# A transformer block on one core: crossed halves of k^T v by transfer for two more batches, and a new order of work behind the first product of h

## The chip, the core and the metric

The kernel runs on one core of a Trainium2 chip. A core has a matrix engine (PE, with weight loads counted apart as PEld), a vector engine (DVE), a scalar engine (ACT), a general engine (POOL) and a queue processor (SP). Each engine works through its own queue strictly in order, and waits for others by semaphores. The metric is device time of one execution in microseconds (us), less is better.

## What is computed

For 8 batches with 8 heads, 576 positions and 64 columns per head:

```
kv  = k^T v                       (64 x 64 per head)
o   = q kv;  x = o / sqrt(mean(o^2) + 1e-6) * g      (x: 576 x 512 per batch)
h   = relu(x @ w_in)              (576 x 1024)
c   = conv over 3 neighbouring positions of h, one weight per column and tap
out = (h * sigmoid(c)) @ w_out    (576 x 512)
```

Inputs and output are float32 in device memory.

## The kernel before

Work is done in bf16, transposed: columns on the 128 partitions, positions along the free dimension. A pair of heads makes one tile t of 0 to 3; the 1024 columns of h are 8 tiles f. The steps below have the names that the kernel gives them; a name with numbers, such as oq.4.0, is the step for batch 4, tile 0.

- **Lq, Lk, Lv** (line 304), **Li**, **Lo**: loads of q, k, v and of both weight matrices, all on POOL's queue, converted on the way.
- **kv** (361): k^T v of a batch on PE, into one bank of PSUM. **kvc** (batches 0, 1) copies it into a block-diagonal tile.
- For batches 2 to 7 the product q kv is made in quarters of PE's array (**oq**, 467). It needs k^T v twice: as it is (**kvn**, a copy from PSUM) and with the halves of the partitions crossed (kvx). The crossed tile is made either by **ky**, two copies from PSUM on ACT or DVE (457), or by **kx**, two transfers on SP's queue out of kvn (452), 32 KB each. Before, batches 2 to 5 use ky, batches 6 and 7 use kx.
- q is transposed on PE (**qt**, **qtp**) and copied from PSUM (**qc**) for batches 0 to 4, and by a DMA transpose on SP's queue (**dq**, 439) for 5 to 7.
- **sq** squares o on ACT; **oc** copies o out of PSUM. The mean of squares comes from a product with ones or selectors (**on**, **ss**), the root from ACT (**nl**, **ln**, 587). For batches 2 to 5 the root is split into two bf16 parts (**sl**) and spread by PE (**sp**, 606); for 6 and 7 it goes through device memory (**fw** writes it, **fr** reads it back broadcast, 613 and 620). **mu**, **mu0** and **muh** on DVE multiply o by root and g, giving x.
- **hm** (643): one tile of h, 8 matmuls of 288 columns; for batches 0 and 1 some are cut in two parts (**ha**, **hb**). **re** is the relu out of PSUM, on ACT or DVE.
- **ta**, **aa**, **ab** (702 to 715): the convolution on DVE. **sg** (748) is the sigmoid on ACT, **mg** (754) multiplies h by it on DVE. Two tiles of h of batch 0 go through PE instead (**dg**, **cm**).
- **om**, **oh** (764, 781): the product with w_out, in tiles of 128 rows and for the first and last pair of batches in two halves of f; **ea**, **eh** copy it out of PSUM on ACT or DVE, **st**, **sh** store it on SP's queue.
- **unread**: matmuls whose result nobody reads; they fill gaps of PE.

Sigmoid and root live in different tables of ACT, and a change of table is an instruction of its own (217); the order holds 12 of them.

The order is written out by hand: a string ORDER of 697 words, which a loop at the end of the kernel runs through one by one, emitting the instructions of each. Each engine's queue has them in just that order, fixed by dependencies from each instruction to the one before it on its engine. In a word, what stands behind `@` are the slots of the buffers that the step takes (PSUM has eight banks, 0 to 7; most products take two that follow each other), and `:1` picks the other engine of a copy or relu:

```
hm.2.4@0  re.2.4      first banks 0 and 1, relu on ACT
re.3.4:1              relu on DVE
```

For re, kvn, ky, oc and ea the plain form is ACT and `:1` DVE; for qc it is the other way round. So a word that is moved, or that takes another slot, changes which wait comes first and who is behind it. A step waits for its inputs, and for the last readers of the slots that it takes.

Of the kernel before, what the change touches and what calls it, by code (L numbers as in the profile page):

```python
# [67 lines left out]
pre@0,0,0 Lq.1.0@1 unread.10.0@1 qt0.0.0@0 qt0.0.1@1 ca.k.0:1 pi ca.v.0:1 qc0.0.0:1@0 unread.2.2@2
kv.0.0.1@3 pn kv.0.1.1@2 kvc.0.0.1.0:1@0 kvc.0.0.1.1 kvc.0.1.1.1 qc0.0.1 unread.3.4@0 kvc.0.1.1.0 ot.0.1@4 ct@1
unread.1.3@0 sq.0.1@0 pg Li.1 unread.2.1@2 on.0.1@0 ot.0.0@6 qt0.0.2@2 pc Li.3 nl.0.1@0 Lk.1.0@1 sq.0.0@0 al.x0@0  # L70
kv.0.2.1@3 kvc.0.2.1.0:1 kvc.0.2.1.1:1 unread.1.1@0 Lv.1.0@1 Li.0 mu0.0.1 on.0.0@0 qc0.0.2:1@0 nl.0.0@1 Lk.1.2 al.h0@0
qt0.0.3@3 ot.0.2@4 sq.0.2@0 kv.0.3.1@2,0 mu0.0.0 qc0.0.3:1 on.0.2@6 unread.3.2@1 kvc.0.3.1.0 kvc.0.3.1.1:1 nl.0.2@0
# [5 lines left out]
sq.1.2@0 sq.1.3@1 Lq.2.0@0 re.0.4 pl on.1.2@6 Lv.2.0@0 aa.0.0 on.1.3@4 nl.1.2@0 ab.0.0 mu0.1.2 nl.1.3@1 hm.0.5@6
qtp.2.0@0 mu0.1.3 re.0.5:1 ha.1.2@4 sg.0.1 hb.1.2 qc.2.0@0 ta.0.4@0 hm.1.6@2 sg.0.3 qtp.2.1@0 Lk.2.0@0 ta.0.5 aa.0.2
sg.0.0 hm.1.1@6 ab.0.2 re.1.2 qc.2.1@1 sg.0.2 ha.1.3@4 ta.1.2@3 re.1.1 sg.0.4 sg.0.5 hb.1.3 mg.0.0 re.1.6 hm.1.7@6  # L80
al.h1@1 kv.2.0.4@0 re.1.7 mg.0.1 re.1.3 kvn.2.0.4:1 ky.2.0.4.1 hm.1.0@2 hm.1.5@6 ky.2.0.4.0 re.1.0 ta.1.6@1 re.1.5
oq.2.0@0 oq.2.1@4 sq.2.0@0 sq.2.1@1 hm.1.4@2 mg.0.2 ta.1.7 ta.1.3 ta.1.0@0 oq.2.2@6 Lv.3.0@1 oc.2.0:1@0 aa.1.3 oc.2.1
oq.2.3@0 Lk.3.0@1 aa.1.1 Lq.3.0@1 kv.3.0.4@4 ta.1.1 sq.2.2@2 sq.2.3@3 ss.2@5 kvn.3.0.4:1 re.1.4 oc.2.2:1@1 qtp.3.0@2
Lo.0 oc.2.3 ky.3.0.4.1 ky.3.0.4.0 ln.8@0 qtp.3.1@0 qc.3.0@0 qc.3.1@1 oq.3.1@6 oq.3.0@2 ab.1.3 oq.3.2@0 sq.3.0@0
oc.3.0@2 aa.1.0 sq.3.1@1 sl.8@0 om.0.1.0@4 Lo.1 oc.3.1 al.x2@0 ab.1.1 sq.3.2@2 om.0.3.0@5 om.0.2.0@2 Lq.4.0@0 oq.3.3@6
ta.1.4@2 om.0.3.4 oc.3.2@3 sq.3.3@3 ta.1.5 om.0.1.4 ab.1.0 oc.3.3 sp.2.0@0,6 ss.3@3 ea.0.3@0 al.x1@1 om.0.0.0@5
ea.0.1@1 ln.1@0 mu.2.0.0 sp.2.1@0,3 sg.1.7 Lv.4.0@0 mu.2.0.1 Lk.4.0@0 om.0.0.4 mu.2.1.0 mu.2.1.1 sl.1@0 qtp.4.0@6
qc.4.0:1@0 hm.2.4@0 om.0.2.4 re.2.4 sg.1.6 sg.1.1 sp.3.1@6,3 sg.1.0 ea.0.0:1@2 mu.3.1.1 mu.3.1.0 Lq.5.0@1 hm.2.2@0
aa.1.2 kv.4.0.4@5 re.2.2 ea.0.2@3 Lv.5.0@1 kvn.4.0.4 sp.3.0@6,3 mu.3.0.1 hm.2.5@0 sg.1.3 mu.3.0.0 ab.1.2 hm.2.7@2
re.2.5 dq.5.0@2 re.2.7 hm.3.5@6 mg.1.0 mg.1.3 hm.3.4@0 ky.4.0.4.0 Lk.5.0@1 sg.1.2 hm.2.6@2 ky.4.0.4.1:1 oq.4.0@4  # L90
re.3.4:1 oq.4.1@0 sg.1.5 ta.2.4@0 re.3.5 dq.5.1@1 re.2.6 ta.2.5 sq.4.0@0 oc.4.0@0 hm.3.1@6 re.3.1 mg.1.1 hm.3.3@2
aa.2.2 qtp.4.1@4 sq.4.1@1 qc.4.1@0 hm.3.6@6 oc.4.1 sg.1.4 mg.1.2 om.0.8.0@0 oq.4.2@4 re.3.3 oq.4.3@2 Lq.7.0@0 re.3.6
Lv.7.0@0 kv.5.0.4@1 sq.4.2@2 oc.4.2@1 ab.2.2 hm.2.3@6 ta.2.6@2 kvn.5.0.4 sq.4.3@3 hm.3.7@4 oc.4.3 ky.5.0.4.0:1
Lk.7.0@0 hm.3.2@2 ky.5.0.4.1:1 sg.2.5 sg.2.4 re.3.7:1 oq.5.0@4 om.0.8.4 sq.5.0@4 om.0.6.0@1 re.2.3:1 oq.5.1@6 re.3.2:1
oc.5.0@2 oq.5.2@2 ea.0.8@4 oq.5.3@4 sq.5.2@5 om.0.4.0@0 oc.5.2@3 om.0.6.4 Lv.6.0@1 mg.2.2 ta.2.7 aa.2.3 om.0.4.4
sq.5.1@6 ss.4@2 oc.5.1 ta.2.2@0 sq.5.3@7 ss.5 om.0.5.0@3 om.0.5.4 hm.2.1@6 ea.0.6@5 ln.2@0 ea.0.4@6 ab.2.3 hm.2.0@0
oc.5.3 st.0.0 ta.2.3 sl.2@0 re.2.1 Lk.6.0@1 ea.0.5@2 aa.2.1 sp.4.0@4,6 mu.4.0.1 om.0.7.0@2 re.2.0 kv.7.0.4@3
sp.4.1@0,6 om.0.7.4 mu.4.0.0 hm.3.0@4 dq.7.0@3 sg.2.7 mu.4.1.1 mu.4.1.0 hm.4.6@6 al.h2@0 sg.2.6 re.3.0 ea.0.7@7
kvn.7.0.4 ab.2.1 mg.2.3 ta.2.0@2 hm.4.0@0 sp.5.0@2,4 kx.7.0.4.1 re.4.6 re.4.0 sg.2.2 hm.4.2@6 hm.4.4@0 mu.5.0.0
mu.5.0.1 ta.2.1 kx.7.0.4.0 st.0.5 re.4.2 st.0.1 Lq.6.0@1 hm.4.5@2 re.4.4 sp.5.1@4,6 re.4.5 kv.6.0.4@0 sg.2.3 oq.7.0@2  # L100
sq.7.0@0 mu.5.1.0 hm.4.3@4 dq.7.1@0 kvn.6.0.4 mu.5.1.1 oc.7.0@0 hm.5.0@6 hm.4.1@0 re.4.3 kx.6.0.4.0 kx.6.0.4.1 re.5.0
dq.6.0@1 re.4.1 oq.7.2@2 aa.2.0 mg.2.1 ab.2.0 sq.7.2@1 oq.7.1@4 oc.7.2:1@1 sg.2.1 sq.7.1@2 hm.5.2@6 hm.5.6@0 re.5.2:1
hm.5.3@2 al.x3@1 oc.7.1 re.5.6:1 dq.6.1@2 hm.5.5@6 oq.7.3@0 re.5.3:1 oq.6.0@2 re.5.5:1 sg.2.0 st.0.3 sq.7.3@3 hm.5.1@4
sq.6.0@4 mg.2.0 st.0.8 hm.5.4@6 oc.6.0@2 re.5.4 re.5.1 om.1.3.0@2 oc.7.3 ta.3.2@0 oq.6.1@4 ta.3.4@2 oq.6.2@6
ea.1.3:1@0 sq.6.1@5 oq.6.3@0 om.1.2.0@3 ta.3.3 sq.6.2@6 sq.6.3@7 ss.7@2 oc.6.2:1@3 ta.3.5 aa.3.1 oc.6.3:1 ss.6@6
st.0.7 om.1.7.0@7 ln.3@0 ab.3.1 oc.6.1 ea.1.2@1 sg.3.2 hm.4.7@4 sg.3.3 aa.3.2 fw.3 st.0.2 ln.4@0 om.1.6.0@6 re.4.7
om.1.4.0@0 ab.3.2 mg.3.1 om.1.8.0@1 hm.5.7@2 sg.3.4 om.1.1.0@4 ea.1.6@2 st.1.2 sg.3.5 fr.6.0@0 ta.3.0@0 om.1.0.0@5
# [10 lines left out]
ea.3.4:1@1 ea.3.0@0 om.3.6.4 st.2.0 om.3.5.4 om.3.3.4 om.3.2.4 st.3.4 st.3.0 ea.3.6:1@2 ea.3.5:1@3 oh.3.8.0@5 st.3.6
om.3.1.4 eh.3.8.0:1@4 st.2.5 ea.3.2@1 st.3.5 st.3.2 ea.3.3@2 st.3.3 om.3.7.4 ea.3.1@0 unread.1.2@0 sh.3.8.0 ea.3.7@0
st.3.1 st.3.7 oh.3.8.1 eh.3.8.1 sh.3.8.1  # L120
"""


# [1 line left out]
def kernel(  # L125
# [216 lines left out]
    def copy(to, fr, on_act):  # L342
        if on_act:
            nc.scalar.activation(to, fr, AX.Copy)  # L344
        else:
            nc.vector.tensor_copy(to, fr)  # L346
# [504 lines left out]
```

## Time and profile before

| | us |
|---|---|
| median of 3 runs | 176.29 |
| lowest and highest run | 176.2, 176.9 |
| span of the profiled execution, from its first to its last instruction | 174.7 |
| PE, DVE, ACT, POOL busy in it | 164.6, 151.8, 144.0, 30.8 |

The profile was taken from one execution of the program; its own time is known only as this span, and the timed runs stand 1.6 us above it. Busy time counts matmuls from start to modelled end, so that small gaps between them can hide in it. The granted clock of PE is full in all of the span but its start and end. DMA is busy until about 90 us, mostly with POOL's loads, and again in parts with stores.

### The profile page before, as it was taken

To read this page: it belongs to the slowest core of one execution; us is meant where nothing else is said; L and a number is where in the kernel's file an instruction comes from. 1 tells how busy PE (TensorE), PEld (TensorE's weight loads), DVE (VectorE), ACT (ScalarE), POOL (GpSimd) and SP (SyncE) were. 2 spreads that over 40 slices of the span, in tenths; PEclk is the share of its full clock that TensorE was granted. 3 is DMA by queue.
4 is the path that set the end of the run, shared out by engine and by line. 5 is a ranking of instruction groups with operands and counts; after the bars stand their busy time and mean duration, and the time that the engine had idled before them with its cause. 6 is when DMAs were issued, how large, how long until landed. Compare 5 with 4: busy or idle time off the path is not lost.

```text
span 174.7 us, 3978 instructions
## 1 busy us (share of the span) xinstructions
PE 164.6 (94%) x1590; PEld 100.1 (57%) x1607; DVE 151.8 (87%) x248; ACT 144.0 (82%) x224; POOL 30.8 (18%) x54
## 2 busy tenths in 40 slices
...
GB/s 151 182 186 198 200 202 203 205 204 204 208 203 205 203 204 164 162 196 191 190 203 234 72 261 6 149 188 181 173 268 161 152 0 4 23 277 235 90 322 196
DMA packets 37450, 30.81 MB, mean 176 GB/s; under 512 B 8608, under 2 KB 32952, under 8 KB 37432
## 3 DMA queue, kind: packets, MB, share of 16 engines
...
q8 instruction: 12, 0.20, 0.4%
...
## 4 chain that ended last, share of the span: by engine, by line
PE 76%; DVE 9%; DMA 4%; POOL 4%; ACT 2%; issue 2%; POOLq 0%; ACTq 0%
PE bank L764 35%; PE bank L643 30%; DMA w_in_sb<-in_moe_w_in_dram 4%; PE bank L361 3%; PE bank L467 2%; DVE taps L703 1%; DVE qT L346 1%; POOL q_sb L245 1%; DVE taps L709 1%; DVE h L754 1%; PE bank L606 1%; DVE taps L702 1%; POOL v_sb L245 1%; POOL k_sb L245 1%; PE bank L781 1%
## 5 line engine op out<-in xcount | busy, mean ns | idle before, releaser
L643 PE MATMUL bank<-xT,w_in_sb 128*128 128x288 bf16 x480 | 63.6, 286 | 0.3 <-ACT root L545 0.2
L764 PE MATMUL bank<-w_out_sb,h 128*128 128x512 bf16 x267 | 62.4, 379 | 0.8 <-issue 0.3
L643 PEld LDWEIGHTS <-w_in_sb 128*128 128x128 bf16 x480 | 46.0, 98 | 14.9 <-issue 1.6
L748 ACT ACTIVATE taps<-taps,cwn 128x1152 bf16<-128x1152 bf16 (+1 forms) x38 | 39.7, 1078 | 7.4 <-DVE taps L715 7.3
L764 PEld LDWEIGHTS <-h 128*128 128x128 bf16 x280 | 26.4, 98 | 31.0 <-issue 1.2
L649 ACT ACTIVATE h<-bank 128x576 bf16<-128x576 f32 x48 | 30.2, 656 | 3.0 <-PE bank L643 2.8
L344 ACT ACTIVATE row<-bank 128x512 f32<-128x512 f32 (+1 forms) x29 | 16.3, 595 | 8.8 <-PE bank L764 6.0
L754 DVE TENSOR_TENSOR h<-h,taps 128x2304 bf16<-128x2304 bf16 (+1 forms) x20 | 22.0, 1109 | 0.6 <-ACT taps L748 0.6
L709 DVE TENSOR_TENSOR taps<-taps 128x2304 bf16<-128x2304 bf16 (+1 forms) x19 | 21.5, 1134 | 0.2
L715 DVE TENSOR_TENSOR taps<-taps,h 128x2304 bf16<-128x2304 bf16 (+1 forms) x19 | 21.5, 1131 | 0.2
L496 ACT ACTIVATE sq<-bank 128x576 bf16<-128x576 f32 x28 | 17.8, 663 | 0.6 <-PE bank L467 0.3
L703 DVE TENSOR_SCALAR taps<-h,cwn 128x1152 bf16<-128x1152 bf16 (+1 forms) x38 | 17.8, 467 | 0.0
L702 DVE TENSOR_SCALAR taps<-h,cwn 128x1152 bf16<-128x1152 bf16 (+1 forms) x38 | 17.4, 457 | 0.3 <-ACT h L649 0.2
L217 ACT ACT_TABLE_LOAD x12 | 15.4, 1283 | 2.6 <-issue 2.4
L651 DVE TENSOR_SCALAR h<-bank 128x576 bf16<-128x576 f32 x16 | 11.8, 752 | 1.7 <-PE bank L643 0.8
L344 ACT ACTIVATE o<-bank 128x576 f32<-128x576 f32 x19 | 12.8, 674 | 0.0
L632 DVE SCALAR_TENSOR_TENSOR xT<-o,cw,bank 128x576 bf16<-128x576 f32 x16 | 12.2, 808 | 0.1
L304 POOL DMA_DIRECT2D q_sb<-in_q_dram x8 | 6.2, 770 | 30.2 <-PE bank L391 29.4
L430 PE MATMUL bank<-fill 128*128 128x512 bf16 x25 | 9.0, 481 | 1.5 <-DVE fill L232 1.5
L346 DVE COPY row<-bank 128x512 f32<-128x512 f32 (+1 forms) x8 | 5.4, 672 | 4.4 <-PE bank L781 2.4
L361 PE MATMUL bank<-v_sb,k_sb 96*64 96x64 bf16 x384 | 8.3, 197 | 0.7 <-ACT sq L496 0.5
L361 PEld LDWEIGHTS <-k_sb 96*64 96x64 bf16 x384 | 7.1, 112 | 2.9 <-issue 2.2
...
## 6 DMA issues: line engine op xcount, KB each, us to landing
...
q_sb<-in_q_dram POOLq DMA_DIRECT2D x4, 144.0 KB, 4.7
```

The lines of the kernel that those rows point to most:

```text
L344: nc.scalar.activation(to, fr, AX.Copy)
L361: nc.tensor.matmul(ps[i][i * D:(i + 1) * D, t - t0, :], k_sb[:, 2 * t + i, r * D:(r + 1) * D], v_sb[:, 2 * t + i, r * D:(r + 1) * D], star ...
L496: nc.scalar.activation(in_order(b, s), product(b, t), AX.Square)
L643: nc.tensor.matmul(ps[:, e, :HS], w_in_sb[:, t, f * P:(f + 1) * P], x[:, t, e * HS:(e + 1) * HS], start=(t == 0), stop=(t == NT - 1))
L649: nc.scalar.activation(to, fr, AX.Relu)
L702: nc.vector.tensor_scalar_mul(tap[:, 0, f % 2, :n, 8:8 + S], h[:, f], cwn[:, 0, f:f + 1])
L703: nc.vector.tensor_scalar_mul(tap[:, 1, f % 2, :n, :S], h[:, f], cwn[:, 2, f:f + 1])
L709: nc.vector.tensor_add(tap[:, 1, :, :n, :S], tap[:, 0, :, :n, 7:7 + S], tap[:, 1, :, :n, 1:1 + S])
L715: nc.vector.tensor_add(y, y, h[:, 2 * j:2 * j + 2])
L748: nc.scalar.activation(y, y, AX.Sigmoid, scale=cwn[:, 1, f:f + 1])
L754: nc.vector.tensor_mul(h, h, T["tap", c, j][:, 1, :, :n, :S])
L764: nc.tensor.matmul(T["om", p, m], h[:, f, m * P:(m + 1) * P], w_out_sb[:, f, :], start=(f == 0), stop=(f == NF - 1))
```

## The change

Batches 4 and 5 make their crossed tile by kx in place of ky. So the four copies go, and SP's queue has four more transfers of 32 KB. The tiles for kvn and kvx of all six batches are now allocated ahead of the steps, and no longer by the first kvn.

The order is the same in its first 69 words, up to the norm of the last tile of batch 0 (`nlh.0.3.1`). Behind that all 628 words are in a new order. Beside the four above, the same steps are in it, and PE has the same 1607 matmuls, 26 of them unread as before. The changes that the prediction speaks of:

- relus that go from DVE to ACT: re.0.2, re.0.3, re.2.3, re.5.3, re.7.0, re.7.2, re.7.6; from ACT to DVE: re.0.6, re.1.2, re.1.4;
- qc.2.1, kvn.2 and kvn.3 go from DVE to ACT; kvn.4, one half of ky.3 and one kvc of batch 1 from ACT to DVE;
- oc: 5.1, 6.1, 7.1 and 7.3 are on DVE, 6.2, 6.3 and 7.2 on ACT; of ea some go each way;
- st.0.0, st.0.1 and st.0.2, the first stores, stand ahead of dq.5.0 on SP's queue, and st.0.8 and st.0.6 ahead of kx.7; before, only st.0.0 is issued before kx.7, behind both dq.5;
- hm.6.5 stands behind the products of batch 7, among those of om.2; the squares of batch 6 stand in the order 0, 1, 3, 2, with both ss behind;
- oh.3.8.0 and oh.3.8.1 stand next to each other at the end; eh.3.8.0 is on ACT, eh.3.8.1 on DVE; one unread matmul is the last on PE.

```diff
 ORDER = """
...
-ot.0.3@2 sqh.0.3.0@0 mu0.0.2 qt.1.0@0 sqh.0.3.1 onh.0.3.0@6 qc.1.0@0 onh.0.3.1 nlh.0.3.0@1 nlh.0.3.1 ha.0.2@4
-muh.0.3.1 ha.0.3@0 muh.0.3.0 ps dg.6 Lv.1.2 hm.0.6@6 dg.7 hb.0.2 re.0.2:1 hm.0.7@2 hb.0.3 re.0.6 cm.0.6@4 sg.0.6@0
...
+ot.0.3@2 sqh.0.3.0@0 mu0.0.2 qt.1.0@0 sqh.0.3.1 onh.0.3.0@6 qc.1.0@0 onh.0.3.1 nlh.0.3.0@1 nlh.0.3.1 dg.7 Lv.1.2 dg.6
+muh.0.3.0 ps ha.0.2@4 ha.0.3@0 muh.0.3.1 hm.0.6@6 re.0.6:1 hb.0.2 hb.0.3 hm.0.7@2 re.0.7:1 re.0.2 ta.0.2@0 cm.0.6@4
...
+qtp.2.1@4 qc.2.1:1@0 al.h1@1 hm.1.1@2 re.1.1 sg.0.3 sg.0.2 qc.2.0@2 re.0.5:1 ta.0.5 aa.0.2 ab.0.2 sg.0.4 ha.1.2@6
+hb.1.2 re.1.2:1 ta.1.2@3 sg.0.0 Lv.2.0@0 mg.0.1 mg.0.0 hm.1.5@4 re.1.5 ha.1.3@2 hb.1.3 re.1.3 ta.1.3 aa.1.1 Lk.2.0@0
+kv.2.0.4@6 ky.2.0.4.1 ky.2.0.4.0 kvn.2.0.4 hm.1.6@0 re.1.6 ta.1.6@1 hm.1.7@2 re.1.7 ta.1.7 aa.1.3 oq.2.0@6 sq.2.0@2
...
+ea.0.2@6 st.0.2 om.0.0.4 ea.0.0@7 sl.1@0 sp.3.1@0,3 mu.3.1.1 mu.3.1.0 hm.2.2@6 re.2.2 Lv.4.0@0 Lk.4.0@0 kv.4.0.4@5
+sg.1.0 sg.1.3 aa.1.2 kvn.4.0.4:1 kx.4.0.4.0 kx.4.0.4.1 sp.3.0@6,0 Lq.5.0@1 sg.1.2 hm.2.7@2 sg.1.7 mu.3.0.1 mu.3.0.0
...
+om.3.1.4 ea.3.1@2 st.3.1 om.3.3.4 ea.3.3:1@1 st.3.3 oh.3.8.0@3 oh.3.8.1 eh.3.8.0@2 sh.3.8.0 eh.3.8.1:1 sh.3.8.1
+unread.1.2@1
...
 """
...
+    for b in QUAD:
+        T["kvn", b] = consts.tile([P, NT, D], BF16, name=f"kvn{b}")
+        T["kvx", b] = consts.tile([P, NT, D], BF16, name=f"kvx{b}")
+
     @op
     def kvn(b, t0, n):
-        if t0 == 0:
-            T["kvn", b] = consts.tile([P, NT, D], BF16, name=f"kvn{b}")
-            T["kvx", b] = consts.tile([P, NT, D], BF16, name=f"kvx{b}")
         copy(T["kvn", b][:, t0:t0 + n], T["kvps", b, t0][0], pick[0] == 0)
```

More of the change, by code (lines that the diff above doesn't have):

```diff
@@ L67 @@
 ORDER = """
[L68 to L72, printed above, removed]
@@ L78 @@
[L78 to L82, printed above, removed]
@@ L83 @@
[L83 to L107, printed above, removed]
@@ L118 @@
[L118 to L120 removed]
+pre@0,0,0 Lq.1.0@1 unread.10.0@1 qt0.0.0@0 qt0.0.1@1 ca.k.0:1 pi ca.v.0:1 qc0.0.0:1@0 unread.2.2@2 kv.0.0.1@3 pn
+kv.0.1.1@2 kvc.0.0.1.0:1@0 kvc.0.0.1.1 kvc.0.1.1.1 qc0.0.1 unread.3.4@0 kvc.0.1.1.0 ot.0.1@4 ct@1 unread.1.3@0
@@ new lines @@
+re.2.7 ab.1.2 st.0.0 hm.2.5@4 re.2.5 Lv.5.0@1 dq.5.0@2 hm.3.5@6 re.3.5 hm.3.4@2 sg.1.5 mg.1.3 mg.1.0 oq.4.0@0 sq.4.0@0
+oc.4.0@3 re.3.4:1 ta.2.4@0 ta.2.5 Lk.5.0@1 hm.2.6@6 oq.4.1@2 hm.3.3@4 qtp.4.1@0 re.2.6 sq.4.1@2 re.3.3 sg.1.4 mg.1.1
+dq.5.1@0 oc.4.1 hm.3.6@6 re.3.6 Lq.7.0@0 hm.3.1@4 re.3.1 qc.4.1@1 oq.4.3@2 oq.4.2@0 sq.4.2@1 kv.5.0.4@6 kvn.5.0.4
+kx.5.0.4.0 kx.5.0.4.1 mg.1.2 sq.4.3@3 oc.4.2@1 oc.4.3 aa.2.2 ab.2.2 sg.2.4 Lk.7.0@0 hm.3.7@4 re.3.7:1 ta.2.6@2 ta.2.7
+aa.2.3 hm.2.3@6 re.2.3 sg.2.5 om.0.8.0@0 hm.3.2@3 re.3.2:1 om.0.8.4 ea.0.8@7 oq.5.1@5 sq.5.1@4 oq.5.0@1 sq.5.0@6
@@ new lines @@
+om.0.6.0@7 om.0.4.0@0 oc.5.0@2 oc.5.1:1 oq.5.3@3 sq.5.3@5 al.x2@0 om.0.4.4 mg.2.2 ta.2.2@0 ta.2.3 ab.2.3 oq.5.2@1
+dq.7.0@1 st.0.8 Lv.7.0@0 sq.5.2@7 om.0.5.0@6 ss.4@5 ss.5 ln.2@0 sl.2@0 dq.7.1@2 aa.2.1 oc.5.2@0 oc.5.3 om.0.6.4
+ea.0.6@7 st.0.6 om.0.5.4 ea.0.5@6 hm.2.1@1 re.2.1 Lv.6.0@1 hm.2.0@4 sp.4.0@2,6 mu.4.0.0 ea.0.4@4 mu.4.0.1 re.2.0
+om.0.7.0@1 sg.2.7 sg.2.6 kv.7.0.4@0 kvn.7.0.4 kx.7.0.4.0 kx.7.0.4.1 sp.4.1@2,4 mu.4.1.1 mu.4.1.0 om.0.7.4 hm.3.0@6
+re.3.0 hm.4.6@2 al.h2@0 re.4.6 ea.0.7@7 hm.4.0@4 hm.4.5@2 re.4.0 ab.2.1 sg.2.2 mg.2.3 ta.2.0@2 sp.5.0@4,0 mu.5.0.1
```

46 lines of the change are left out of this document (32 added, 14 removed).

## The prediction

> **What bounds the kernel now.** I read the page's first lines, then the busy time in four stretches that I cut where the chain that ended last changes engine: the first product of h, the last normalised tile of batch 1, the first product of batch 2, the last gate.
>
> ```profile
> span 174.7 us, 3978 instructions
> PE 164.6 (94%) x1590; PEld 100.1 (57%) x1607; DVE 151.8 (87%) x248; ACT 144.0 (82%) x224; POOL 30.8 (18%) x54
> ```
> ```profile
> 16.60:31.60 15.00, 13.23 (x157) 9.29 (x160) 13.01 (x26) 13.09 (x27) 7.82 (x18) 1.00 1.34 202
> 31.60:56.50 24.90, 23.39 (x313) 15.29 (x314) 24.73 (x50) 24.70 (x41) 5.03 (x7) 1.00 1.30 205
> 56.50:167.60 111.10, 110.31 (x943) 66.55 (x952) 105.54 (x144) 93.29 (x135) 4.91 (x6) 1.00 0.75 161
> ```
>
> After the length of a stretch stand the busy us of PE, PEld, DVE, ACT and POOL, PE's clock and the DMA share. From 31.6 to 56.5 DVE is idle for 24.90 - 24.73 = 0.17 us and ACT for 0.20, while PE has gaps. From 56.5 to 167.6 PE is idle for 111.10 - 110.31 = 0.79 us in 111. So there are two regimes, and the chain of waits in order of time shows the same:
>
> ```profile
> 31.59 1.54 DVE xT L565 x2
> ...
> 47.29 0.75 DVE qT L346
> ...
> 56.50 0.98 PE bank L643 x8
> ...
> 124.15 13.81 PE bank L643 x112
> ...
> 147.52 10.74 PE bank L764 x49
> ...
> 171.36 0.28 ACT row L344
> ```
>
> Up to about 47 us nearly every piece of the chain is DVE's, from 56.5 on nearly every one PE's. The new order issues the same matmuls. Hence what it can gain is bounded: the 0.8 us of PE's gaps in the long second regime, and before it DVE's gaps: 2.0 us (15.00 - 13.01) and 0.17. Past 56.5 us, work taken from DVE or ACT shortens nothing unless it closes one of those 0.8 us.
>
> **The change, part by part.** *Copies that become transfers.* Four copies of crossed halves go, one from ACT and three from DVE; four transfers on SP come, two for batch 4 and two for batch 5.
>
> ```profile
> L344 ACT ACTIVATE kvx<-bank 64x256 bf16<-64x256 f32 x5 | 1.9, 378 | 0.1
> L346 DVE CAST kvx<-bank 64x256 bf16<-64x256 f32 x3 | 1.3, 420 | 0.1
> L346 DVE CAST kvn<-bank 128x256 bf16<-128x256 f32 x2 | 0.8, 414 | 0.0
> ```
> ```profile
> L452 SPq DMA_DIRECT2D kvx<-kvn x4: 467/568/589, 90.4 to 97.3; - x4
> ```
> ```profile
> kvx<-kvn SPq DMA_DIRECT2D x2, 32.0 KB, 3.0
> ```
> ```profile
> 59.65 0.95 PE L361 MATMUL bank<-v_sb,k_sb 96*64 96x64 bf16 x48
> ```
> ```profile
> 65.78 0.31 PE L467 MATMUL bank<-qT,kvn 64*64 64x288 bf16 x1
> ```
>
> That takes 3 x 0.42 us off DVE and 0.38 off ACT. All of it lies past 56.5 us, where PE hides them; I cost it at nothing. The price is a delay: the product oq.4.0 needs both transferred halves. They are issued after kvn.4 on DVE, which follows kv.4. That ended at 60.60 us (59.65 + 0.95) and will end near 60.9, with the later start of the second regime worked out below; behind one add on DVE kvn.4 then ends near 61.65. Two issues of 0.57 us put the second at 62.25. The 3.0 us are the landing of the pair of batch 7, issued between 90.4 and 91.0 with loads still running, so it lands near 65.25. The old oq.4.0 began at 65.78, with one product of h (0.98) more ahead of it and a wait of 0.2; PE will be there at 65.78 - 0.98 - 0.2 + 0.45 = 65.05. So it waits 0.2 to 0.3 us, with all of PE's queue behind it. Bounds: 0 if it lands as fast as the later pair (2.0), 4 us if it takes the 7.4 of the transposes that SP issued at 62 us under full load. I take 0.25, since copies of the same form are the nearest row.
>
> ```profile
> kvx<-kvn SPq DMA_DIRECT2D x2, 32.0 KB, 2.0
> ```
> ```profile
> qT<-q_sb SPq DMA_TRANSPOSE x2, 7.4
> ```
>
> The Trainium skill, "DMA: Bandwidth & Descriptors", section "Anatomy of one DMA", gives a fixed cost of some 2.0 us and bytes over 436 GB/s; by that, an estimate, 32 KB land 2.1 us after issue and this wait would be zero. The unloaded pair agrees with 2.0, the loaded pair differs with 3.0.
>
> *The first regime: same work, other waits.* Counting the order up to the last normalisation of batch 2, DVE loses two relus (re.0.2, re.0.3), one qT copy and two kvn to ACT, and gains three relus, one crossed half and one copy of 0.2 us.
>
> ```profile
> L649 ACT ACTIVATE h<-bank 128x576 bf16<-128x576 f32 x48 | 30.2, 656 | 3.0 <-PE bank L643 2.8
> L651 DVE TENSOR_SCALAR h<-bank 128x576 bf16<-128x576 f32 x16 | 11.8, 752 | 1.7 <-PE bank L643 0.8
> L346 DVE COPY qT<-bank 128x1152 bf16<-128x1152 bf16 x7 | 5.2, 747 | 0.0
> L344 ACT ACTIVATE qT<-bank 128x1152 bf16<-128x1152 bf16 x1 | 1.1, 1130 | 0.0
> L748 ACT ACTIVATE taps<-taps,cwn 128x576 bf16<-128x576 bf16 x14 | 10.2, 774 | 0.0
> ```
>
> For DVE: +3 x 0.75 + 0.42 + 0.22 - 2 x 0.75 - 0.75 - 2 x 0.41 = -0.2 us. For ACT about +0.6. So the saturated engine has no less to do, and only its waits count. Up to mu0.1.3 the norms of batch 1 still go one by one through PE, ACT and DVE; following them I get its end at 33.05 us against 33.13 (the first row of the chain: 31.59 + 1.54), with 0.1 us more of DVE's work behind it: 0.2 us gained. Then ACT is the late one. From 33.45 it has to do sg.0.1, the qT copy (1.13, which DVE did before), re.1.1, and four sigmoids up to sg.0.0, ending at 38.4 (durations above, each start some 0.1 us ahead of the end before it, as the starts in the traced queue are). DVE comes to mg.0.0, which needs sg.0.0, at 38.15: 0.25 waited. ta.1.3 needs re.1.3, behind re.1.5 on ACT: 0.3. ta.1.6 needs re.1.6, which now stands behind three copies of k^T v of batch 2 on ACT: 0.25. In before this stretch has no such wait. Together 0.8, less the 0.2 and less small gaps that the old order has too; DVE ends the qT copies of batch 3 near 48.5 instead of 48.04 (47.29 + 0.75). What follows (sl.8, the taps, the four mu of batch 2) is the same work on a busy DVE, so the second regime starts 0.3 to 0.45 us later. I take 0.45; ends: -0.2 if none of the three waits comes, +0.9 if ACT is late again at sl.8.
>
> *The second regime.* PE's gaps of 0.79 us may all go. New ones: the 0.25 of oq.4.0; about 0.35 between 76 and 100 us, where hm.2.1, sp.4.0, sp.5.0 and sp.5.1 take banks that ACT's relus and copies have only just left, by my sums with under 0.1 us to spare (nothing to 0.8); ss.6, which comes after sq.6.2, the last of three squares on ACT (0.25); and the factors of batch 7.
>
> ```profile
> 107.91 1.19 ACT L496 ACTIVATE sq<-bank 128x576 bf16<-128x576 f32 x2
> ...
> 117.16 0.50 ACT L587 ACTIVATE rs<-bank,eps_sb 128x288 f32<-128x288 f32 x1
> ```
> ```profile
> 121.34 2.59 SPq L620 DMA_DIRECT2D factor<-factor  x4
> ```
> ```profile
> 127.96 1.55 DVE L628 SCALAR_TENSOR_TENSOR xT<-o,cw,factor 128x576 bf16<-128x576 f32 x2 [0.46 <-DMA factor<-factor]
> ```
> ```profile
> 131.71 1.08 PEld L643 LDWEIGHTS <-w_in_sb 128*128 128x128 bf16 x9
> ```
>
> DVE already waits 0.46 us for these factors. In the new order ln.4 comes some 1.4 us later: the squares of batch 6, which ended at 109.10, end near 110.2, and one more tile is evicted ahead of it (0.5, less a 0.2 wait that goes). The factors' reads, issued at 121.34 behind the write of ln.4's result, and their landing move by as much, so the first mu of batch 7 starts near 129.4, the next waits for the reads of the other half, issued 1.3 (half of 2.59) later, and the third ends near 132.2. The first product of batch 7 is due earlier than before: hm.6.5 is put behind it, so 131.71 - 0.98 + 0.45 + 0.6 (the waits ahead) = 131.8 us, and it needs that third mu. I take 0.45 us (0 to 1.5). New waits: 0.25 + 0.35 + 0.25 + 0.45 = 1.3, less 0.8: +0.5.
>
> *The tail.* At the end the two parts of the last tile stand next to each other.
>
> ```profile
> 170.72 0.61 PE L781 MATMUL bank<-w_out_sb,h 128*128 128x128 bf16 x8
> 171.75 0.41 SPq L795 DMA_DIRECT2D out_dram<-row  x1
> ```
>
> Before, the last store is issued 0.42 us after PE's last matmul (171.33). After, SP has two issues in a row behind it, the first for the large part that ACT evicts in about 0.5 us: the last issue comes 0.6 us after it: +0.2 (-0.3 to +0.4). The fill that closes PE's queue is behind nothing that is read.
>
> **Sum:** 0.45 + 0.5 + 0.2 = 1.15 us on a span of 174.7: 175.85. The median of the three runs, 176.29, lies 1.6 us above the profiled span; with the same 1.6 around it, 177.4 us.
>
> **Rivals.** *DVE's relief counts (faster).* The gate of the last quarter of h ends the vector work and holds PE up:
>
> ```profile
> 161.30 1.36 DVE L754 TENSOR_TENSOR h<-h,taps 128x2304 bf16<-128x2304 bf16 x1 [0.60 <-ACT taps L748]
> 162.71 4.43 PEld L764 LDWEIGHTS <-h 128*128 128x128 bf16 x22 [0.41 <-DVE h L754]
> ```
>
> DVE's queue ahead of it becomes 4 us shorter (five relus, three crossed halves, and the 0.2 above, less a kvn and an output copy). If DVE paced the second regime through many such small waits, its relief would give back PE's whole 0.79 us, with the 0.2 gained up to 33 us and no wait behind it 1.0: 175.3; with half of DVE's 2.0 us before 31.6 as well, 174.3. For it: DVE is busy for 105.54 of 111.1 us. Against: PE is busy for 110.31, and this wait is 0.41 us.
>
> *No change.* The waits on ACT near 40 us are absorbed, the factors land in time, and the 0.8 us go as others come: 175.5 to 177.1.
>
> *Transfers late (slower still).* Three stores of 256 KB move to 54 to 63 us, into the stretch with a DMA share of 1.30; at the 205 GB/s of that row each delays the loads by 1.3 us. From about 3 us on kv.7 and the transposes of batch 6, with kx.6 behind them on SP, would be late: 178.8 to 180. The Trainium skill, same page, section "Queues, rings and completion order", has each engine take turns between queues by packets; by that the stores take their share at once, and the loads pay. No row of before shows stores against full loads.
>
> **How the numbers follow.** My sum 0.42 (176.9 to 178.6), no change 0.28, faster 0.18, late transfers 0.12. Half a per cent, 0.88 us, is about what a measurement of this kernel tells from none: faster 0.18, same 0.28, slower 0.54. The range 175.7 to 179.4 leaves out the far half of the faster case and most of the late one.
>
> **What would show it.** Right: DVE gaps near 38 to 42 us; the first product of batch 2 at 56.7 to 57; the second pair of kvx landing within 0.5 us of oq.4.0; ln.4 past 118 and a PE gap ahead of the first product of batch 7. Wrong: PE reaching the first product of batch 2 before 56.2, or PE idle for under 0.5 us past it.

## The result, and the profile after

The changed kernel takes **188.99 us** (median of 6 runs, 186.87 to 189.37), the kernel before in the same series 176.56 (6 runs, 176.2 to 177.07). The ratio is 1.068, with a 95% interval of 1.063 to 1.073. So it is slower by 12.4 us, where 1.1 were forecast, and the time lies 9.6 us above the range. Some executions of a kernel come out slower than the rest; medians below are of all runs, while ratios and intervals leave the slow ones out.

The first lines of the page of the changed kernel, and two of the four stretches into which the prediction cut the kernel before (behind the length of a stretch stand the busy us of PE, PEld, DVE, ACT, POOL, then PE's clock and the DMA share):

```profile
span 185.1 us, 4002 instructions
PE 167.7 (91%) x1607; PEld 99.9 (54%) x1607; DVE 150.4 (81%) x243; ACT 146.6 (79%) x225; POOL 30.5 (16%) x54
```
```profile
31.60:56.50 24.90, 23.08 (x300) 14.35 (x299) 23.38 (x46) 23.73 (x40) 4.98 (x7) 1.00 1.30 204
56.50:167.60 111.10, 103.97 (x922) 63.14 (x923) 98.95 (x134) 92.53 (x135) 4.70 (x6) 1.00 0.69 143
```

In the same 111.10 us of the second regime PE is now idle for 7.13 us (111.10 - 103.97), and was for 0.79. In the first, DVE is idle for 1.52 us (24.90 - 23.38), and was for 0.17. Both regimes lost the tightness that the prediction had read there. Five rows of the timeline show the large holes (start, length, and in brackets the idle time just before and what ended it); the first of them only marks where the second regime starts:

```profile
57.81 0.66 PE L644 MATMUL bank<-xT,w_in_sb 128*128 128x288 bf16 x4
```
```profile
68.76 0.31 PE L468 MATMUL bank<-qT,kvx 64*64 64x288 bf16 x2 [1.61 <-DMA kvx<-kvn]
```
```profile
81.81 0.31 PE L468 MATMUL bank<-qT,kvx 64*64 64x288 bf16 x2 [1.58 <-DMA kvx<-kvn]
```
```profile
93.02 0.30 PE L607 MATMUL bank<-wparts,spread 32*128 32x288 bf16 x4 [2.11 <-ACT h L650]
```
```profile
141.13 0.66 PE L644 MATMUL bank<-xT,w_in_sb 128*128 128x288 bf16 x4 [1.35 <-DVE xT L629]
```

The first product of batch 2 begins at 57.81 us instead of 56.34. Then PE stands at oq.4.0, at oq.5.1, at sp.4.0 and at hm.7.0. Who is behind each is in the chain that ended last (start, length, piece; `...` stands for pieces left out):

```profile
54.62 5.87 DMA out_dram<-row
...
63.22 0.55 SPq L453
...
63.81 4.91 DMA kvx<-kvn
...
80.95 10.29 DMA out_dram<-row
...
91.84 0.59 ACT row L344
92.43 0.55 ACT h L650
...
126.95 3.23 DMA factor<-rs
...
132.22 7.21 DMA factor<-factor
...
139.53 1.56 DVE xT L629 x2
```

Four DMA pieces have taken over what was PE's chain. The two transfers of 32 KB for batch 4 need 4.9 us to land (those for batch 5, which are not among these rows, 5.7). One store of 256 KB needs 10.3. Behind that one stands ACT:

```profile
91.34 1.09 ACT L344 ACTIVATE row<-bank 128x512 f32<-128x512 f32 x2 [2.20 <-DMA out_dram<-row]
92.31 0.66 ACT L650 ACTIVATE h<-bank 128x576 bf16<-128x576 f32 x1
```

ea.0.6 takes row slot 7, from which st.0.8 still reads until 91.24 (80.95 + 10.29). So ACT waits, re.2.1 behind it is late, and sp.4.0 on PE waits for the bank that this relu reads. The row slots, which are the `@` of ea, are in no step of the prediction.

The holes of PE in this execution are 1.9 (oq.4.0), 1.9 (oq.5.1), 2.2 (sp.4.0) and 1.6 us (hm.7.0), each as PE's advance in the trace less its work: 7.6 us. The idle times in the rows are shorter, since the modelled end of the matmul ahead covers the start of a hole (the first matmul of oq.4.0 starts at 66.85, the next at 68.76). With the 1.5 of the later start and 0.4 at the end they make 9.5 of the 10.4 by which the spans differ (185.1 - 174.7); the rest is not located. The profiled execution, 186.87 us, is the shortest of the six. The other five show a mean granted clock of PE of 0.979 to 0.982, the profiled one 0.996; that goes with the last 2 us of the median. Where in these five the clock fell is not on record.

### The profile page after: what moved, and what is told of

Read it like the earlier page. It is cut to its first block, busy times and chain, and to the rows that moved or that the text cites. A ratio compares the mean times of both kernels' runs of the same rounds, so it can differ in the third digit from the quotient of the medians.

```text
span 185.1 us, 4002 instructions
## 1 busy us (share of the span) xinstructions
PE 167.7 (91%) x1607; PEld 99.9 (54%) x1607; DVE 150.4 (81%) x243; ACT 146.6 (79%) x225; POOL 30.5 (16%) x54
## 3 DMA queue, kind: packets, MB, share of 16 engines
q0 software_dynamic: 21760, 15.96, 56.6%
## 4 chain that ended last, share of the span: by engine, by line
PE 50%; DMA 19%; ACT 16%; issue 5%; DVE 4%; SPq 2%; POOL 1%; ACTq 0%; DVEq 0%; POOLq 0%
PE bank L765 20%; PE bank L644 19%; DMA out_dram<-row 9%; DMA factor<-factor 4%; ACT L217 3%; DMA kvx<-kvn 3%; ACT sq L497 2%; ACT taps L749 2%; PE bank L361 2%; DMA v_sb<-in_v_dram 2%; ACT h L650 2%; PE bank L468 2%; DMA factor<-rs 2%; PE bank L430 2%; ACT row L344 1%
## 5 line engine op out<-in xcount | busy, mean ns | idle before, releaser
L765 PE MATMUL bank<-w_out_sb,h 128*128 128x512 bf16 x280 | 63.7, 379 | 0.0
L749 ACT ACTIVATE taps<-taps,cwn 128x1152 bf16<-128x1152 bf16 (+1 forms) x38 | 39.2, 1081 | 1.3 <-DVE taps L716 1.3
L650 ACT ACTIVATE h<-bank 128x576 bf16<-128x576 f32 x52 | 32.6, 654 | 4.5 <-PE bank L644 3.9
L344 ACT ACTIVATE row<-bank 128x512 f32<-128x512 f32 (+1 forms) x28 | 15.8, 593 | 15.4 <-DMA out_dram<-row 7.8
L344 ACT ACTIVATE o<-bank 128x576 f32<-128x576 f32 x18 | 11.4, 661 | 0.0
L652 DVE TENSOR_SCALAR h<-bank 128x576 bf16<-128x576 f32 x12 | 9.0, 754 | 1.9 <-PE bank L644 1.7
```

Of the source, the lines that this page charges most:

```text
L650: nc.scalar.activation(to, fr, AX.Relu)
L749: nc.scalar.activation(y, y, AX.Sigmoid, scale=cwn[:, 1, f:f + 1])
L765: nc.tensor.matmul(T["om", p, m], h[:, f, m * P:(m + 1) * P], w_out_sb[:, f, :], start=(f == 0), stop=(f == NF - 1))
```

## The experiments

The theory after this reading, **A**: the transfers land late since POOL's loads hold the DMA engines (until about 97 us in this trace), and the store for the same reason; every other wait follows from these. Ratios are to the kernel before, run beside each. In the edits below only words of ORDER change, unless something else is shown.

### 1. The copies back in the transfers' places

```diff
-kx.4.0.4.0 kx.4.0.4.1
+ky.4.0.4.0 ky.4.0.4.1:1
-kx.5.0.4.0 kx.5.0.4.1
+ky.5.0.4.0:1 ky.5.0.4.1:1
```

> The changed kernel with the four transfers for batches 4 and 5 turned back into copies (ky), at the same places of the order; nothing else. Theory A (the transfers land late, and PE waits for them): the two waits of PE at oq.4.0 (2.0 us) and oq.5.1 (1.8 us) go, the copies cost ACT and DVE 1.6 us that nothing waits for; the profiled span falls from 185.1 to 181 to 182.5. Rival B (PE would have waited there anyway, for ACT and DVE, which the new order runs late): the span stays within 1 us of 185.1 and the wait at oq.4.0 is for an engine instead of a transfer.

188.18 us, 1.065 (1.062 to 1.069). The expected gain did not come. The two waits for kvx are gone, but DVE meets its copies of batch 5 too early in its queue:

```profile
DVE kvx L346 <- ACT kvn L344: 2.8, 1, 2.8
```

A relu of DVE (re.3.7) is late in turn, and PE waits 2.0 us for it; the wait at sp.4.0 stays as well (2.5 us). So the places were badly chosen, and the run tells little of the transfers.

### 2. The transfers alone, in the old order

```diff
-kvn.4.0.4
+kvn.4.0.4 kx.4.0.4.0 kx.4.0.4.1
-kvn.5.0.4
+kvn.5.0.4 kx.5.0.4.0 kx.5.0.4.1
-ky.4.0.4.0 ... ky.4.0.4.1:1 ... ky.5.0.4.0:1 ... ky.5.0.4.1:1
```

> The kernel before, in its old order, with the crossed halves of batches 4 and 5 by transfer, issued right behind kvn, so that for batch 4 nothing stands ahead of them on SP's queue; POOL's loads run as before. Theory A1 (a small transfer takes 5 to 6 us because the loads hold the DMA engines): both pairs land 5 to 6 us after issue, PE waits 1 to 1.5 us at oq.4.0 and 3 to 4 us at oq.5.0, and the time is 4 to 5.5 us above the kernel before. Theory A2 (it takes that long only because stores and DMA transposes stand ahead of it on SP's queue): the pair of batch 4 lands within 3 us, no wait at oq.4.0, and the time is at most 1.5 us above the kernel before.

186.80 us, 1.059 (1.055 to 1.063). The transfers alone, with nothing else of the change, cost 10.5 us, far more than either theory had (4 to 5.5, and at most 1.5). They are issued at 61.15 us on an empty queue of SP, and PE comes to oq.4.0 at 65.5:

```profile
PEld L467 <- DMA kvx<-kvn: 7.1, 2, 3.7
```
```profile
DMA to landing us min/median/max: 1.7/3.4/7.2
```

So a free queue does not make them land early; that it is the load which delays them is shown by experiment 13. The waits are 7 us in all; two stretches behind them show where much of the rest goes:

```profile
69.00:73.00 4.00, 3.99 (x31) 2.58 (x32) 0.22 (x1) 2.42 (x5) 0.00 (x0) 0.64 0.45 91
...
83.40:87.00 3.60, 3.27 (x10) 1.04 (x8) 3.60 (x6) 1.79 (x3) 0.00 (x0) 0.50 1.27 203
```

In both, behind a hole of over 3 us, PE's clock (the third number from the end) is at 0.64 and 0.50. PE counts as busy and does half the work.

### 3. The row slots apart

```diff
-ea.0.2@6 ... ea.0.6@7 ... ea.0.7@7 ... ea.0.8@7
+ea.0.2@0 ... ea.0.6@2 ... ea.0.7@3 ... ea.0.8@5
```

> The changed kernel with other slots for four of the output rows of the first pair (ea.0.2, ea.0.6, ea.0.7, ea.0.8), so that no copy out of PSUM has to wait for an earlier store to land; every step stays where it is. Theory A: ACT's waits for stores (7.8 us in three) go, with them PE's wait of 2.1 us at sp.4.0, which stood behind re.2.1 on ACT; the span falls by 2 to 4 us to 181 to 183. Rival B (ACT's wait was slack): less than 0.7 us.

185.40 us, 1.053 (1.047 to 1.058): 3.6 us less than the changed kernel, for four numbers of slots, as theory A had it (2 to 4). Between the two profiled executions the difference is 1.3 us (183.8, 185.1); the other runs differ in PE's clock too (0.99 to 1.00 here, about 0.98 there). The waits of ACT for stores, first in the changed kernel and then here:

```profile
ACT row L344 <- DMA out_dram<-row: 7.8, 3, 5.1
```
```profile
ACT row L344 <- DMA out_dram<-row: 5.1, 1, 5.1
```

The one that is left lies among the last tiles, near 175 us, where PE does not wait for it. The other two, 0.4 and 2.2 us near 60 and 90, are gone, and sp.4.0 does not wait.

### 4. Three stores behind the factors of batch 7

```diff
-st.1.1 ... st.0.5 ... st.1.6 ... fr.7.1@0
+fr.7.1@0 st.1.1 st.0.5 st.1.6
```

> The changed kernel with three stores (st.1.1, st.0.5, st.1.6) moved behind the reads of the factors of batch 7 on SP's queue, nothing else. Theory A (the 768 KB of stores ahead of them make the factors late): the factors land 5 to 5.5 us after their issue instead of 7.2, PE's wait of 1.6 us ahead of the first product of batch 7 falls to under 0.5, the span falls by 1 to 1.6 us. Rival B (ln.4 itself is late and sets it): the span changes by less than 0.5 us.

196.63 us, 1.112 (1.108 to 1.116): far off. The stores, issued later, hold their row slots longer, and ea.1.4 needs slot 3 of st.1.6:

```profile
ACT row L344 <- DMA out_dram<-row: 16.1, 4, 8.3
...
PE bank L644 <- ACT row L344: 8.2, 1, 8.2
```

The edit meant to free the factors, and showed the same mechanism as experiment 3 from the other side, at 8.2 us of PE. The factors gained little by it. The last of their reads lands 6.9 us after its issue (7.2 in the changed kernel, 5 to 5.5 expected), and DVE waits nearly as long for it, first in the changed kernel and then here:

```profile
139.53 2.28 DVE L629 SCALAR_TENSOR_TENSOR xT<-o,cw,factor 128x576 bf16<-128x576 f32 x3 [1.69 <-DMA factor<-factor]
```
```profile
142.25 2.28 DVE L629 SCALAR_TENSOR_TENSOR xT<-o,cw,factor 128x576 bf16<-128x576 f32 x3 [1.54 <-DMA factor<-factor]
```

So it makes little difference whether the three stores are issued ahead of these reads or right behind them.

### 5. The copies at better places

```diff
-kx.4.0.4.0 kx.4.0.4.1 ... kx.5.0.4.0 kx.5.0.4.1 ... ab.2.2
+ky.4.0.4.0 ky.4.0.4.1:1 ... ky.5.0.4.0 ... ab.2.2 ky.5.0.4.1:1
```

> The changed kernel, with copies in place of the four transfers again, now where the engines do not wait in front of them: for batch 4 one copy on ACT and one on DVE in the transfers' places, for batch 5 one on ACT right behind kvn.5 and one on DVE behind ab.2.2. Theory A (the landing of the four transfers under POOL's loads costs 1.9 us at oq.4.0 and 1.6 at oq.5.1, and PE's clock a little more): 3.5 to 4.5 us under the changed kernel, 184.5 to 185.5. Rival (the copies only take the waits to ACT and DVE, as in the first experiment, since these have no time for them in this order): 187.5 to 189.

189.87 us, 1.077 (1.073 to 1.081). Theory A missed here, and the trace says why:

```profile
91.86 1.08 ACT L344 ACTIVATE row<-bank 128x512 f32<-128x512 f32 x2 [4.21 <-DMA out_dram<-row]
```
```profile
93.54 0.43 PE L607 MATMUL bank<-wparts,spread 32*128 32x288 bf16 x4 [4.12 <-ACT h L650]
```

PE reaches sp.4.0 1.5 us earlier, and waits there for 4.12 us instead of 2.11, until the same moment (93.54, before 93.02). The store sets it. The wait for transfers and the wait for the store lie one behind the other on PE, and the later one hides what the earlier one loses: they do not add. With the longer hole the mean clock of PE is at 0.981 in the profiled execution as well, at 0.50 from 92 to 98 us.

### 6 and 7. Copies and slots together, and two more edits

Experiment 6 has the edits of 5 and 3. Experiment 7 has these and

```diff
-kvn.3.0.4 ky.3.0.4.0 ky.3.0.4.1:1
+kvn.3.0.4:1 ky.3.0.4.0 ky.3.0.4.1
-hm.6.6@4 ... hm.6.5@6 re.6.5
+hm.6.5@6 re.6.5 hm.6.6@4
```

> The same copies, and the row slots of the third experiment (ea.0.2 on 0, ea.0.6 on 2, ea.0.7 on 3, ea.0.8 on 5), so that ACT no longer waits ahead of ea.0.6 for a store to land. Theory A (the two costs lie in different places and add): 184.5 to 185.5, less the 3.6 that the slots gave alone: 181 to 182. Rival (both waits hide the same lateness of ACT, so that the second edit gives little beyond the first): 183.5 to 185.

> The same, and two more: kvn.3 on DVE and both crossed halves of batch 3 on ACT, as before the change; and hm.6.5 and its relu back ahead of the products of batch 7, so that PE has 0.98 us more to do while the factors of batch 7 are under way. Theory A: 0.6 to 1.2 from the first, 0.9 to 1.0 from the second: 179 to 180.5. Rival (PE's waits in the first regime come from ACT's work as a whole, and hm.7.0 waits longer instead): no more than 0.5 us under the kernel without these two.

184.24 us, 1.047 (1.040 to 1.054), and 182.46 us, 1.037 (1.032 to 1.042). The first time lies in the rival's range (183.5 to 185), but not for the rival's reason: beyond the copies alone the slots give over 5 us. Beyond the slots alone (1.053) the copies give about 1 us, which the intervals do not tell from nothing. What they save at oq.4.0 and oq.5.1 they cost in good part at hm.2.5, hm.3.5 and hm.2.3, for which the rows of experiment 6 name DVE:

```profile
PE bank L644 <- DVE kvx L346: 1.1, 2, 0.6
PE bank L644 <- DVE xT L633: 0.6, 1, 0.6
```

At these places the new order has no time left for the copies. The two more edits are worth 1.8 us together, as theory A had it (1.5 to 2.2), from a higher level. In the trace the stretch from hm.6.3 to om.2.3 is 0.6 us shorter for the same work, and the way from hm.0.5 to the first product of batch 2 is 26.05 us instead of 26.35. The two profiled executions differ by only 0.6 us in all (180.8, 181.4); the rest of the 1.8 is not located.

### 8. The two edits alone

> The changed kernel with the last two edits alone (kvn.3 on DVE and both crossed halves of batch 3 on ACT; hm.6.5 back ahead of the products of batch 7). Theory A: 1.5 to 2.2 us under the changed kernel, 186.8 to 187.5; the first product of batch 2 starts at 56.6 to 57.2 instead of 57.77, and PE waits 0.6 to 0.8 ahead of hm.7.0 instead of 1.64. Rival: within 0.5 us of the changed kernel, as the waits of 66 to 93 us, which stay, take the gain of the first regime.

The changed kernel with the second diff of experiment 7 only: 186.94 us, 1.062 (1.058 to 1.066), against 1.068: 2.0 us less, as theory A had it, though not by the parts that it named. From hm.6.3 to om.2.3 1.3 us are gained, and PE does not wait ahead of hm.7.0. The first regime gains 0.3 again, from hm.0.5 on (26.05 against 26.36), not the 0.6 to 1.2 expected. In the profiled execution hm.0.5 itself comes 1.85 us later than in that of the changed kernel (33.30, 31.45), behind a stretch with PE's clock at half, so that the first product of batch 2 came at 59.3 and not at 56.6 to 57.2.

### 9 to 11. Shorter loads, with a filling that spoils the times

```diff
     def load(x, b, t0):
...
+        if b >= 5:
+            nc.gpsimd.dma_start(out=qkv[x, b][:, 0:1, :], in_=heads(x, b, 0, 1))
+            nc.gpsimd.memset(qkv[x, b][:, 1:8, :], 0.0)
+            return
```

It stands in the kernel of experiment 2, in the changed kernel and in the kernel before.

> The old order with the four transfers (the second experiment's kernel), whose loads of q, k and v of batches 5, 6 and 7 bring only the first of eight heads; POOL fills the rest with zeros. So DMA has an eighth of its loads behind batch 4, and the results of batches 5 to 7 are not those of the reference. Theory A (the transfers land late because POOL's loads hold the DMA engines): the pairs land in under 2.5 us instead of 3.4 to 7.2, PE waits under 0.5 us ahead of oq.4.0 and oq.5.0 instead of 3.3 and 3.9, and 175.5 to 178.5 us in all instead of 186.8. Rival (the transfers themselves, two per batch behind one copy on a strict queue, take that long): pairs of 4 to 7 us again, and 184 or more.

> The changed kernel with the same shortened loads. Theory A (loads are the common cause of the late transfers and of the store that holds row slot 7): no wait ahead of oq.4.0 and oq.5.1 (1.9 and 1.6 in the changed kernel), the store st.0.8 lands in 3 to 5 us instead of 10.3, sp.4.0 waits under 0.5 instead of 2.2, and the time is 180 to 182.5 us: 189.0 less the 5.7 of these waits and up to 2 of PE's clock, with the 1.5 of the first regime and the factors of batch 7 left. Rival (the store is late because it stands behind the transposes on SP's queue, and ACT because of its own work): the transfers' waits go, but sp.4.0 still waits 2 us or more, 184 to 187.

> The kernel before with the same shortened loads, as what the two others are to be held against. PE has hardly a gap behind 56.5 us, so that lighter loads can give nothing there: 175 to 176.5 us. If POOL's filling disturbs DVE, up to 178.

195.91 us, 1.111 (1.104 to 1.118); 203.05, 1.147 (1.137 to 1.157); 196.78, 1.115 (1.107 to 1.122). All three are far beyond what was expected, the one that has nothing of the change too. The filling is at fault. While POOL fills, three operations of DVE of 128 x 1152, of 0.51 us each in the kernel before, take 4.2 in the eleventh kernel (POOL fills tiles of k and v in the same way):

```profile
L306 POOL MEMSET q_sb<- 96x2688 bf16 x3 | 7.3, 2429 | 0.0
```
```profile
L706 DVE TENSOR_SCALAR taps<-h,cwn 128x1152 bf16<-128x1152 bf16 x3 | 12.7, 4236 | 0.0
```

So the times say nothing of the transfers. Their landing does, in the ninth kernel and the tenth:

```profile
DMA to landing us min/median/max: 1.7/1.9/2.5
```
```profile
DMA to landing us min/median/max: 1.7/1.9/2.6
```

### 12. Transfers, slots apart and the two edits

> The changed kernel with its transfers, the row slots of the third experiment and the two late edits (batch 3's copies as before the change, hm.6.5 ahead of the products of batch 7): the seventh kernel without its copies. Theory A: the transfers cost 0.95 and 1.7 us with the rows apart, the copies 2.1 at hm.2.5, hm.3.5 and hm.2.3, so both are about even: 182 to 184. Rival (PE's clock falls behind each wait for a transfer, and makes them dearer): 185 to 186.5.

184.37 us, 1.043 (1.033 to 1.053): just above theory A's 182 to 184 by the median of all four runs, within it by that of the three on which the ratio rests (183.1), and below the rival. With the slots apart it makes little difference in the new order whether the four halves are copied (experiment 7, 1.037) or transferred.

### 13 to 15. The loads of batches 5 to 7 left out

```diff
     def load(x, b, t0):
+        if b >= 5:
+            qkv[x, b] = qkv[x, 4]
+            slots.clear()
+            return
```

It stands in the kernel of experiment 2, in the changed kernel and in the kernel before.

> The old order with the four transfers, with the loads of q, k and v of batches 5, 6 and 7 left out and nothing in their place: these batches use the tiles of batch 4, so their results are not the reference's. Theory A (the loads make the transfers late): both pairs land in about 2 us, PE waits under 0.6 us ahead of oq.4.0 and oq.5.0 (3.3 and 3.9 with loads), and 175.5 to 177.5 us in all, within 1.5 of the fifteenth kernel, where the transfers cost 10.5 with the loads. Rival (transfers cost PE their wait in any case): 180 or more.

> The changed kernel with the same loads left out. Theory A (the loads are the common cause of the late transfers and of the store that holds the row slot): waits at oq.4.0, oq.5.1 and sp.4.0 under 0.5 us each, st.0.8 lands in under 5 us instead of 10.3, and 179 to 182 us. Rival (the order itself has ACT late at sp.4.0, whatever the loads): sp.4.0 waits 1.5 us or more, 183 to 186.

> The kernel before with the same loads left out, as what the two others are held against: 175 to 176.5 us, since PE has next to no gaps behind 56.5 us that lighter loads could close.

177.16 us, 1.004 (1.000 to 1.009); 181.05, 1.028 (1.020 to 1.036); 176.47, 1.000 (0.995 to 1.004). All three times are as theory A had them. Without these loads the transfers alone cost 0.7 us (177.16 - 176.47) instead of 10.5, and the whole change 4.6 (181.05 - 176.47) instead of 12.4. Landing and wait of the transfers in the thirteenth, then in the changed order (the fourteenth) their landing, that of st.0.8, and the second regime:

```profile
DMA to landing us min/median/max: 1.8/2.0/3.9
```
```profile
PEld L471 <- DMA kvx<-kvn: 0.5, 2, 0.3
```
```profile
DMA to landing us min/median/max: 1.7/1.8/2.3
```
```profile
out_dram<-row SPq DMA_DIRECT2D x1, 256.0 KB, 2.2
```
```profile
56.50:167.60 111.10, 109.70 (x955) 65.66 (x955) 103.18 (x138) 95.85 (x137) 0.00 (x0) 1.00 0.39 109
```

PE's idle time of 7.13 us in the second regime is down to 1.40, the store lands in 2.2 us instead of 10.3, and sp.4.0 does not wait, though slots, stores and queues are those of the changed kernel. So nearly two thirds of the 12.4 us (7.8) stand and fall with the loads. Of the 4.6 that stay, the later start of batch 2 is the first (40.1 us from hm.0.6 to hm.2.4, against 38.2 in the fifteenth), and hm.7.0 the second, nearly unchanged:

```profile
134.95 1.25 PE L648 MATMUL bank<-xT,w_in_sb 128*128 128x288 bf16 x8 [1.30 <-DVE xT L633]
```

### 16. The first regime's engines in the old order

```diff
-re.0.2:1 ... re.0.3:1 ... re.0.6 ... re.1.2 ... re.1.4
+re.0.2 ... re.0.3 ... re.0.6:1 ... re.1.2:1 ... re.1.4:1
-qc.2.1@1 ... kvn.2.0.4:1 ... kvn.3.0.4:1 ... ky.3.0.4.1
+qc.2.1:1@1 ... kvn.2.0.4 ... kvn.3.0.4 ... ky.3.0.4.1:1
```

> The kernel before, its order unchanged, with the relus and copies of batches 0 to 3 on the engines that the change gives them: re.0.2, re.0.3, qc.2.1, kvn.2 and kvn.3 on ACT; re.0.6, re.1.2, re.1.4 and one crossed half of batch 3 on DVE. Theory A (the first regime's 1.5 us come from DVE waiting for ACT because of these moves): 0.8 to 1.5 us slower, 176.9 to 177.8, and DVE idle for 1 us or more from 31.6 to 56.5. Rival (they come from the order of the steps): within 0.5 us of the kernel before.

The edit has the moves of the first regime that the section on the change lists, but for the kvc of batch 1. 181.43 us, 1.027 (1.018 to 1.036): 4.8 us slower, three times theory A's most. From hm.0.6 to hm.2.4 it takes 42.2 us (38.3 before, 40.2 in the changed kernel), and DVE's largest wait, ahead of 33 us, is of the kind that the prediction counted, a tap that waits for a relu on ACT:

```profile
DVE taps L702 <- ACT h L649: 2.4, 2, 2.2
```

So the moves between the engines are dear where the order around them is not made for them: 3.9 us in this stretch, where moves and new order together cost 1.9. A part of the 3.9 is PE's clock, which is at 0.61 from 52 to 56 us of this execution. Which part of the changed kernel's later start is the moves and which the order, this does not settle.

## Why the prediction was wrong, point by point

The direction held, the size did not. By the prediction's own terms:

| term | forecast, us | measured, us |
|---|---|---|
| first product of batch 2 later | +0.45 (-0.2 to +0.9) | +1.5 (+1.9 counted from hm.0.6) |
| oq.4.0 waits for the transfers | +0.25 (0 to 4) | +1.9 |
| oq.5.1 waits for them | not in the sum | +1.9 |
| sp.4.0 and others, 76 to 100 us | +0.35 (0 to 0.8) | +2.2 |
| ss.6 waits for sq.6.2 | +0.25 | no wait of PE in the rows |
| hm.7.0 waits for the factors | +0.45 (0 to 1.5) | +1.6 |
| old gaps of PE that go | -0.8 | some -0.3 (0.5 us of idle time is left beside the four holes) |
| tail | +0.2 | +0.4 (3.8 us behind the end of the last matmul that is read, before 3.4) |
| PE's clock, at half in stretches | not in the sum | some 2 in the median |

**Two regimes: right.** Work taken off DVE behind 56.5 us gave nothing: DVE's busy time fell from 151.8 to 150.4 us while the span grew by 10.4.

**Copies that become transfers: the step that failed.** It said: "I take 0.25, since copies of the same form are the nearest row". That row was a pair issued at 90.4 us, some 2 us before the loads ended. The other row, DMA transposes that SP issued at 62 us with 7.4 us to land, stood there as the upper bound only, for the form of its transfer. It was the nearer one: what counted most was for how long the loads would still hold the DMA engines. The pair of batch 4 landed in 4.9 us, that of batch 5 in 5.7. The pairs issued at 98 us or later, with the loads over, took 1.9:

```profile
kvx<-kvn SPq DMA_DIRECT2D x2, 32.0 KB, 1.9
```

Experiments 13 to 15 show it in both orders, the old and the new. Beside that, only oq.4.0 was costed. The same wait of batch 5 was left out, though POOL's loads ran past 90 us in the kernel before.

The Trainium skill, "DMA: Bandwidth & Descriptors", section "Anatomy of one DMA", with its 2.0 us and bytes over 436 GB/s (which the Trainium skill fits to DMAs that POOL issues; these are SP's), is borne out where the loads are over or left out (medians of 1.8 to 2.0, the longest 3.9) and is off by a factor of two to three where they run (4.9 and 5.7). The prediction had set that figure beside the two rows, and did not draw from the difference that load was the variable.

**First regime: right in kind, too small.** Up to the norms of batch 1 the reckoning holds (mu0.1.3 ends at 32.97, forecast 33.05; sg.0.0 at 38.36, forecast 38.4). Of the three waits counted behind that, one came, at ta.1.6 (the first row below, 0.29 us, forecast 0.25); at mg.0.0 and at ta.1.3 DVE's queue runs on without a gap. And a wait came that was not counted: ky.3 is split over two engines, and DVE's half waits for ACT's, which comes behind ACT's kvn.3:

```profile
41.21 0.37 DVE L703 TENSOR_SCALAR taps<-h,cwn 128x576 bf16<-128x576 bf16 x1 [0.29 <-ACT h L650]
...
46.33 0.42 DVE L346 CAST kvx<-bank 64x256 bf16<-64x256 f32 x1 [0.56 <-ACT kvx L344]
```

That the saturated engine has no less to do, and that only its waits count, fits the 1.52 us that DVE is idle in this stretch. But the count of the waits was wrong in both directions, and the two rows make 0.85 of the 1.52; two waits of 0.2 us for PE and small gaps make the rest.

**76 to 100 us: the right place, the wrong cause.** The prediction had sp.4.0 behind ACT's relus "with under 0.1 us to spare", and no look at what ACT itself could wait for. Row slot 7 goes from ea.0.8 to ea.0.6 there, and the store between them takes 10.3 us to land. Experiment 3 takes this wait away alone, and without the loads it goes as well.

**Factors of batch 7: right in kind, just above the upper end.** The wait came where it was worked out, 1.6 us against 0 to 1.5. The last of the reads takes 7.2 us to land, where it took 6.5 in the kernel before; the prediction moved the landing and did not lengthen it. The wait stays without the loads of batches 5 to 7, so that these are not its cause. With the three stores behind the reads instead of ahead of them it hardly changes either (6.9 us of landing in experiment 4). In experiment 8, with hm.6.5 back in its old place, PE does not wait for them; in experiment 7 it waits 0.9 us. What makes the landing longer stays open.

**Rivals.** DVE's relief and no change fell. "Transfers late" named the early stores and 178.8 to 180 us, but had the loads suffer from the stores. In the main it was the reverse: the stores paid (10.3 us for one, 5.9 for another), and through their slots ACT, and PE. The loads landed later too (the last 22.2 us after its issue, before 19.5), but PE did not wait for kv.7's data nor for the transposes of batch 6. Both signs that the prediction named for being wrong looked to the fast side, and neither came; none of its signs could tell a time that was far too long.

**What was in no term: PE's clock.** In experiment 2 it is at 0.64 and 0.50 in the 4 us behind holes of over 3 us. The Trainium skill, "TensorE: Matmul & The Clock Gate", Part 1, has the clock at half after an idle window of about 3.4 us, in windows that run freely. Experiment 2 agrees. Experiment 8 differs: its profiled execution has two stretches of some 3.4 us at half clock, one with no idle time of PE over 0.8 us in the 5 us ahead of it (the first row), one behind a hole of 2.35 us at oq.5.1 (the others):

```profile
29.00:32.00 3.00, 3.00 (x14) 1.63 (x14) 2.33 (x4) 1.22 (x3) 3.00 (x5) 0.50 1.32 204
84.00:86.50 2.50, 2.50 (x7) 0.85 (x8) 2.03 (x3) 1.52 (x3) 0.00 (x0) 0.50 1.28 189
```
```profile
83.29 0.45 PE L468 MATMUL bank<-qT,kvx 64*64 64x288 bf16 x2 [2.04 <-DMA kvx<-kvn]
```

Two stretches of 3.4 us at half clock are worth 3.4 of 184.9 us, which is the 0.018 that its mean clock of 0.982 lacks. The profiled execution of the changed kernel shows none of them behind its holes of 1.6 to 2.2 us, and the five others have a mean of 0.979 to 0.982. So an estimate from experiment 8 is two stretches in each of these; whether they stand behind the new holes or in the first regime, as one in experiment 8 does, is not shown.
